# One MLP matmul or two in every open slot, gelu's ScalarE passes in halves taken from a queue, and query copies on ScalarE in mixer stage two

## The chip, the cores and the metric

The kernel runs on one core of a Trainium2 chip. The metric is device microseconds (us) of one execution. The engines are TensorE (PE, its weight loads shown as PEld), VectorE (DVE), ScalarE (ACT), GpSimd (POOL) and SyncE (SP), which only issues transfers.

## The reference

Attention of 2048 tokens over 32 heads with a given key and value cache, gated by a mixer block with an MLP; `D` is 512, `F` 1792, the inputs are bf16.

```python
xn = _layernorm(A_x)
# A: attention with cached keys and values
q = (xn @ wq) as 32 heads of 128
p = _softmax(q @ k_cache.T * 128 ** -0.5)
s = (p @ v_cache, heads side by side) @ wo
# B: mixer and MLP
h = _gelu(_layernorm(xn) @ w1)
hs = concat(four column groups of h, shifted by +1, -1, +2, -2 tokens) @ w2
x1 = xn + hs
h2 = _gelu(_layernorm(x1) @ w3) @ w4
g = _silu(x1 + h2)
return A_x + s * g
```

The gelu is the tanh approximation.

## The kernel before

Everything runs in one stream of 1024 slots, written out by the main loop (line 766). A unit is one head with 512 queries; there are 128 units (8 groups of 4 heads, 4 query tiles, 4 heads) and each has `SPU` = 8 slots. Slot `n` is slot `p = n % 8` of unit `u = n // 8`. All compute instructions are pinned to the order in which the Python code emits them, and each engine runs its own instructions in that order.

In each slot `s_slot` (line 187) emits two score matmuls, 128 keys by 512 queries each, into a PSUM tile `ps_s` of two banks, and one exponential of 1024 columns on ScalarE that turns it into half of a `pT` tile. The pool `psS` has two such tiles, so the scores of slot n+2 wait until the exponential of slot n has read its tile. `pv_slot` (line 216) emits two matmuls with the values, a lag of 5 to 10 slots behind; the lag grows by one at slots 260, 264, 268, 272 and 276, which have no value matmuls. So a slot has four matmuls of 512 columns, and some have more, here called extras:

- slots 0 and 1: two each for the queries of unit u+2 (`q_mm`, line 171; `q_copy`, line 179, brings them from the bank `xa` to SBUF in slot 2, on VectorE for nearly all units);
- slots 4 and 5: two each for the output projection (`wo_mm`, line 290), added to `s_acc` by VectorE in slot 6 (`wo_post`);
- slots 2, 3, 6 and 7, the open slots: the MLP. A window is a pair of them (2, 3 or 6, 7), numbered `w = 2u` or `2u + 1`. The MLP is a list `chunks`; each chunk has two parts, for the two slots of one window, with two matmuls each (two or three in `m4_chunk`). At the start of a window the loop compares `done` chunks with a straight line from window 10 to window 240 and takes the next chunk, or none, if the line is not passed yet.

The chunks are, in order: stage one (`m1_chunk`, h = gelu(... w1), 16 chunks), stage two (`m2_chunk`, the shifted product with w2 and the residual, 16) and, for each of four token tiles, 14 chunks of `m3_chunk` (gelu(... w3)) and 12 of `m4_chunk` (the product with w4, three chunks for each 128 tokens). All accumulate in the one bank `xm`.

`gelu_chunk` (line 502) evicts its bank on ScalarE (`pre`, line 512). After each second chunk `gelu_pair` (line 477) puts four steps on 1024 columns at fixed distances from slot n of the eviction: `square` on ScalarE one slot later, `poly` on VectorE at n+3, `tanh` on ScalarE at n+5, `last` on VectorE at n+7. `at(n, fn)` (line 134) sets a step for slot n; the loop runs a slot's steps behind its own. `soft` (line 137) moves a step to slot 3, 5 or 7 of a unit. `m4_chunk` ends with one `x2` on VectorE, a tanh on ScalarE three slots later (line 664) and `silu` on VectorE.

VectorE also sums the exponentials (lines 204 to 214), normalises the outputs (line 278 and 285), and writes the final result. POOL issues the MLP's transfers, SyncE those of attention.

Of the kernel before, what the change touches and what calls it, by code (L numbers as in the profile page):

```python
# [8 lines left out]
ACT = mybir.ActivationFunctionType  # L9
# [8 lines left out]
def kernel(  # L18
# [92 lines left out]
    o_d = {qt: dsp.tile([P, HG, 512], BF16, name=f"o_d{qt}") for qt in range(QT)}  # L111
    g_d = [dsp.tile([P, D], BF16, name=f"g_d{t}") for t in range(NT)]

    def mm(out, lhsT, rhs, start, stop):
        pin(nc.tensor.matmul(out=out, lhsT=lhsT, rhs=rhs, start=start, stop=stop))  # L115

    def rsqrt(out, var):
# [16 lines left out]
    def at(n, fn):  # L134
        todo[n].append(fn)
# [42 lines left out]

    def q_copy(u):
        qT = qtp.tile([P, 512], BF16, name="qT")  # L180
        if u > QUIET + 1:
            pin(nc.scalar.activation(out=qT[:], in_=st[u].pop("psq")[:], func=ACT.Identity))
        else:
            pin(nc.vector.tensor_copy(out=qT[:], in_=st[u].pop("psq")[:]))  # L184
        st[u]["qT"] = qT
# [287 lines left out]


    mlp = {}

    def gelu_pair(pre, dest, n):
        sq = gtp.tile([P, 2, 512], BF16, name="sq")
        f2 = "p a f -> p (a f)"

        def square():
            pin(nc.scalar.activation(  # L482
                out=sq[:], in_=pre[:], func=ACT.Square, scale=GELU_A ** 0.5))

        def poly():
            pin(nc.vector.scalar_tensor_tensor(
                out=sq[:].rearrange(f2), in0=sq[:].rearrange(f2), scalar=1.0,
                in1=pre[:].rearrange(f2), op0=ALU.add, op1=ALU.mult))

        def tanh():  # L490
            pin(nc.scalar.activation(out=sq[:], in_=sq[:], func=ACT.Tanh, scale=GELU_C))  # L491

        def last():
            pin(nc.vector.scalar_tensor_tensor(
                out=dest, in0=sq[:], scalar=1.0, in1=pre[:], op0=ALU.add, op1=ALU.mult))

        at(n + 1, square)
        at(n + 3, poly)
        at(n + 5, tanh)
        at(n + 7, last)  # L500

    def gelu_chunk(lhs, rhs, j, key, dest):
        def run(i, n):
            if i == 0:
                mlp["ps"] = psX.tile([P, 512], FP32, tag="xm", name="ps_m")
            for dc in (2 * i, 2 * i + 1):
                mm(mlp["ps"][:], lhs(dc), rhs(dc), dc == 0, dc == DC - 1)
            if i == 1:
                if j == 0:
                    mlp["pre"] = gtp.tile([P, 2, 512], BF16, name="pre")  # L510
                pre = mlp["pre"]
                pin(nc.scalar.activation(out=pre[:, j, :], in_=mlp["ps"][:], func=ACT.Identity))  # L512
                if j == 1:
                    gelu_pair(pre, dest(), n)
        return run

    ph = ExitStack()
# [32 lines left out]
    def m2_chunk(t):  # L550
        def run(i, n):
            if i == 0:
                mlp["ps"] = psX.tile([P, 512], FP32, tag="xm", name="ps_m")
                xr = mlp["xr"] = mlp.pop("xnext")
                at(n + 1 if n % SPU == 2 else n, lambda: norm1(t, xr[:], xr[:]))
                if t + 1 < NT:
                    xn_load(t + 1)
            for jc in (2 * i, 2 * i + 1):
                c0 = BASE_J[jc] + t * P - SHIFT[jc]
                mm(mlp["ps"][:], hT[:, jc, c0:c0 + P], w2_sb[:, jc, :], jc == 0, jc == DC - 1)  # L560
            if i == 1:
                ps, xr = mlp["ps"], mlp["xr"]

                def x1():
                    pin(nc.vector.scalar_tensor_tensor(
                        out=xr[:], in0=ps[:], scalar=0.5, in1=xr[:], op0=ALU.mult, op1=ALU.add))
                    nc.gpsimd.dma_start(out=x1_d[t][:], in_=xr[:])

                def stats():
                    bn = smp.tile([P, nc.vector.BN_STATS_DIM], FP32, name="bn")  # L570
                    pin(nc.vector.bn_stats(out=bn[:], in_=xr[:]))
                    pin(nc.vector.bn_aggr(out=mv2[:, t, :], in_=bn[:]))
                    rsqrt(rstd2[:, t:t + 1], mv2[:, t, 1:2])

                at(evict(n), x1)
                at(soft(n + 2), stats)
        return run

    def ph2_open():
        ph.close()  # L580
        ph2 = ph.enter_context(pool("ph2", reuse_waits="tile"))
        mlp.update(ph2=ph2, w4={}, h2={})

    def w4_load(fc):
        mlp["w4"][fc] = mlp["ph2"].tile([P, D], BF16, name=f"w4_sb{fc}")
# [25 lines left out]
    def m3_chunk(c, fc):  # L611
        def dest():
            mlp["h2"][fc // 2] = mlp["ph2"].tile([P, 2, 512], BF16, tag="h2T", bufs=FC // 2, name="h2T")
            return mlp["h2"][fc // 2][:]

        inner = gelu_chunk(
            lambda dc: mlp["w3"][:, dc, (fc % 2) * P:(fc % 2 + 1) * P],
            lambda dc: mlp["xn2T"][:, dc, :], fc % 2, None, dest)

        def run(i, n):  # L620
            if i == 0 and fc % 2 == 0:
                mlp["w3"] = mlp["w3next"].pop((c, fc))
            if i == 0 and c == 0:
                w4_load(fc)
            inner(i, n)
            if i == 1 and fc % 2 == 1:
                w3_prefetch()
        return run

    w3_order = deque((c, fc) for c in range(QT) for fc in range(0, FC, 2))  # L630
# [6 lines left out]
            pin(nc.gpsimd.dma_start(out=w[:], in_=w3_v[:, :, fc * P:(fc + 2) * P]))  # L637
            mlp["w3next"][(c, fc)] = w

    M4 = [range(0, 4), range(4, 9), range(9, 14)]  # L640

    def m4_chunk(t, part):
        fcs = list(M4[part])
        ts = t % 4

        def run(i, n):
            if part == 0 and i == 0:
                mlp["ps"] = psX.tile([P, 512], FP32, tag="xm", name="ps_m")
                mlp["xr"] = tokp.tile([P, D], BF16, tag="tb", bufs=4, name="xr")
                nc.gpsimd.dma_start(out=mlp["xr"][:], in_=x1_d[t][:])  # L650
            h = (len(fcs) + 1) // 2
            for fc in (fcs[:h], fcs[h:])[i]:
                mm(mlp["ps"][:], mlp["h2"][fc // 2][:, fc % 2, ts * P:(ts + 1) * P],
                   mlp["w4"][fc][:], fc == 0, fc == FC - 1)
            if part == 2 and i == 1:
                ps, xr = mlp["ps"], mlp["xr"]
                th = tokp.tile([P, D], BF16, tag="th", bufs=1, name="th")

                def x2():
                    pin(nc.vector.scalar_tensor_tensor(  # L660
                        out=xr[:], in0=ps[:], scalar=0.5, in1=xr[:], op0=ALU.mult, op1=ALU.add))

                def tanh():
                    pin(nc.scalar.activation(out=th[:], in_=xr[:], func=ACT.Tanh, scale=0.5))

                def silu():
                    pin(nc.vector.scalar_tensor_tensor(  # L667
                        out=xr[:], in0=th[:], scalar=1.0, in1=xr[:], op0=ALU.add, op1=ALU.mult))
                    nc.gpsimd.dma_start(out=g_d[t][:], in_=xr[:])  # L669

                at(evict(n), x2)
                at(n + 3, tanh)
                at(soft(n + 5), silu)
        return run

    chunks = deque()
# [12 lines left out]
    for c in range(QT):  # L689
        for fc in range(FC):  # L690
            chunks.append(m3_chunk(c, fc))
        if c + 1 < QT:
            hooks[len(chunks)] = lambda n, c=c: ln2(c + 1, n)
        for ts in range(4):
            for part in range(3):
                chunks.append(m4_chunk(c * 4 + ts, part))
    NCH = len(chunks)
    W0, W1 = 10, 2 * (NU - 8)
    done = 0
    window = {}  # L700


    for t, eng in enumerate([nc.sync, nc.scalar, nc.sync, nc.scalar]):
# [61 lines left out]

    for n in range(NS):
        u, p = divmod(n, SPU)
        s_slot(u, p)
        lag = next(v for lim, v in LAGS if n < lim)
        while pv_done <= n - lag:  # L770
# [14 lines left out]
        if p == 0 and u >= 1:  # L785
            add_next(u - 1, 3)
            if not turned(u - 1):
                fold(u - 1)
        if p == 2 and HG - 1 <= u < NU - 2:
            q_copy(u + 2)  # L790
        if p == 2 and u >= 1 and turned(u - 1):
            fold(u - 1)
# [31 lines left out]
            pin(nc.vector.tensor_tensor(out=a[:, 0:2, :], in0=a[:, 0:2, :], in1=a[:, 2:4, :], op=ALU.add))  # L824
        if p == 6 and u < QUIET:
            add_next(u, 2)
        if p in (2, 3, 6, 7):
            w = 2 * u + (p >= 4)
            i = p % 2
            if i == 0:  # L830
                want = -(-(w + 1 - W0) * NCH // (W1 - W0)) if w >= W0 else 0
                window.pop("run", None)
                if done < min(want, NCH):
                    if done in hooks:
                        hooks.pop(done)(n)
                    window["run"] = chunks.popleft()
                    done += 1
            if "run" in window:
                window["run"](i, n)
        for fn in todo.pop(n, ()):  # L840
            fn()
        if p == SPU - 1 and u >= 2 and turned(u - 2):
            normed(u - 2)
        if p == SPU - 1 and u == T1 + 1:
            bcast(T1)
    late = [fn for n in sorted(todo) for fn in todo[n]]
    assert min(todo) >= NS and not chunks and len(wo_todo) == 1
    U = NU - 1
# [79 lines left out]
```

## Time and profile before

| what | value |
|---|---|
| median of 3 runs | 1270.44 us (1269.98 to 1271.06) |
| span of the profiled execution | 1268.2 us |
| granted TensorE clock, mean | 0.999 |
| ACT waiting for `ps_s` scores | 122.6 us, 426 times, longest 1.1 us |
| DVE waiting for `ps_wo` (line 352) | 54.5 us, 73 times |
| DMA | 123.03 MB, mean 97 GB/s |

The profile lists, for every engine, its busy time, and for each group of instructions (line, engine, operation, output and input tiles, shape) how many there are, their busy time, the mean length of one and the idle time of the engine just before them with what ended it. `L115` is the one line that emits all matmuls, so there the tiles tell them apart. Successive instructions of an engine overlap in the records, so the time from one start to the next is shorter than the length of one. A row of the timeline has its start, its length, the engine and line, the operation and the number merged into it.

### The profile page before, as it was taken

The page shows a single profiled execution, that of the slowest core. Times are in us where ns is not written, and L with a number is a line of the kernel's source. Part 1 is how long each engine was busy: PE and PEld are TensorE (multiplying, and loading weights), DVE is VectorE, ACT ScalarE, POOL GpSimd, SP SyncE. Part 2 cuts the span into 40 slices and gives each one's busy share as a digit, 9 for nine tenths or more (in the row PEclk, how much of TensorE's full clock was granted, in tenths as well). Part 3 has the DMA queues.
Part 4 walks back from the last instruction along what each step waited for, and adds up shares of the span by engine and source line. Part 5 has one row for each costly group of instructions (what it writes and reads, how often), then busy time and mean ns, then how long its engine had stood idle before and what let it go on. Part 6 is the DMA issues. An engine that isn't in the chain of part 4 may idle for free.

```text
span 1268.2 us, 16717 instructions
## 1 busy us (share of the span) xinstructions
PE 1256.0 (99%) x5984; PEld 602.0 (47%) x5984; DVE 1091.5 (86%) x1494; ACT 1112.5 (88%) x1200; POOL 140.9 (11%) x239
## 2 busy tenths in 40 slices
PE   9999999999999999999999999999999999999998
PEld 5444444444444444444444444444444444444444
DVE  7888879898899888889898888988888899888887
ACT  7899998888999988899998889998888999988893
POOL 4420003333110010000000000000000000000111
PEclk9999999999999999999999999999999999999999
DMA  9633344355544564244554344534545344552532
GB/s 184 136 92 68 55 80 98 94 126 118 129 96 85 112 121 96 58 96 97 96 101 94 76 93 96 105 74 91 103 95 112 68 73 87 107 123 50 153 77 68
DMA packets 219876, 123.03 MB, mean 97 GB/s; under 512 B 171600, under 2 KB 196816, under 8 KB 219792
## 3 DMA queue, kind: packets, MB, share of 16 engines
q1 hardware_dynamic: 210688, 96.72, 38.9%
q0 software_dynamic: 8672, 24.91, 7.7%
q8 instruction: 46, 0.75, 0.3%
q14 instruction: 38, 0.31, 0.1%
q10 hardware_dynamic: 432, 0.33, 0.1%
HBM read 82.58 MB, written 7.60 MB: 71 GB/s over the span
## 4 chain that ended last, share of the span: by engine, by line
PE 78%; ACT 12%; DVE 7%; issue 2%; DMA 1%; POOL 0%; SPq 0%; DVEq 0%; ACTq 0%
PE ps_s L115 29%; PE ps_o L115 27%; ACT pT L198 9%; PE ps_m L115 8%; PE ps_wo L115 7%; PE ps_q L115 7%; DVE acc L209 2%; ACT pre L512 1%; ACT sq L482 1%; DMA rb<-dr 1%; ACT sq L491 1%; DVE oT L278 1%; DMA dr<-rc 1%; DVE acc L204 0%; PE ps_sum L115 0%
## 5 line engine op out<-in xcount | busy, mean ns | idle before, releaser
L198 ACT ACTIVATE pT<-ps_s 128x1024 bf16<-128x1024 f32 x1024 | 1013.0, 1033 | 132.3 <-PE ps_s L115 122.6
L115 PE MATMUL ps_s<-qT,kT 128*128 128x512 bf16 x2048 | 608.9, 379 | 2.8 <-ACT pT L198 0.9
L115 PE MATMUL ps_o<-pT,vb 128*128 128x512 bf16 x2048 | 608.2, 379 | 0.5 <-DMA vb<-in_A_v_cache_dram 0.4
L115 PEld LDWEIGHTS <-kT 128*128 128x128 bf16 x2048 | 229.8, 113 | 235.4 <-issue 23.5
L209 DVE TENSOR_TENSOR acc<-acc,pT 128x2048 bf16<-128x2048 bf16 x254 | 307.6, 1211 | 22.7 <-ACT pT L198 20.8
L115 PEld LDWEIGHTS <-vb 128*128 128x128 bf16 x2048 | 199.5, 98 | 226.2 <-DMA vb<-in_A_v_cache_dram 0.9
L204 DVE TENSOR_TENSOR acc<-pT 128x2048 bf16<-128x2048 bf16 x128 | 156.2, 1220 | 25.9 <-ACT pT L198 24.9
L115 PE MATMUL ps_q<-xnT,wq_h 128*128 128x512 bf16 (+1 forms) x524 | 152.2, 374 | 0.6 <-ACT xnT L450 0.4
L115 PE MATMUL ps_wo<-wo_h,oT 128*128 128x512 bf16 (+1 forms) x476 | 140.2, 378 | 0.0
L352 DVE TENSOR_TENSOR s_acc<-ps_wo,s_acc 128x512 f32<-128x512 f32 x100 | 68.9, 689 | 54.6 <-PE ps_wo L115 54.5
L184 DVE CAST qT<-ps_q 128x512 bf16<-128x512 f32 x122 | 83.7, 686 | 14.1 <-PE ps_q L115 14.0
L278 DVE TENSOR_TENSOR oT<-ps_o,rb 128x512 bf16<-128x512 f32 x86 | 92.2, 1073 | 1.0 <-DMA rb<-dr 1.0
L213 DVE TENSOR_TENSOR acc<-acc 128x1024 bf16<-128x1024 bf16 x127 | 87.0, 685 | 1.4
L115 PEld LDWEIGHTS <-wq_h 128*128 128x128 bf16 x524 | 50.8, 98 | 61.0 <-issue 1.2
L115 PEld LDWEIGHTS <-oT 128*128 128x128 bf16 x484 | 47.3, 98 | 56.6 <-DVE oT L285 0.5
L115 PE MATMUL ps_m<-xn2T,w_sb 128*128 128x512 bf16 x224 | 66.7, 379 | 0.0
L115 PE MATMUL ps_m<-w_sb,h2T 128*128 128x512 bf16 x224 | 64.1, 379 | 0.0
L637 POOL DMA_DIRECT2D w_sb<-in_B_w_dram x28 | 21.1, 755 | 362.0 <-PE ps_m L115 327.1
L251 DVE TENSOR_REDUCE sm<-accT 128x4 f32<-128x512 bf16 x86 | 58.6, 681 | 0.1
L214 DVE TENSOR_TENSOR acc<-acc 128x512 bf16<-128x512 bf16 x127 | 54.0, 425 | 4.4
L669 POOL DMA_DIRECT2D g_d<-xr x16 | 8.8, 547 | 319.5 <-DVE xr L667 319.5
L512 ACT ACTIVATE pre<-ps_m 128x512 bf16<-128x512 f32 x72 | 42.8, 594 | 1.3 <-PE ps_m L115 1.3
(89 smaller groups left out, 611.0 us busy)
## 6 DMA issues: line engine op xcount, KB each, us to landing
rb<-dr SPq DMA_DIRECT2D x128, 256.0 KB, 4.2
vb<-in_A_v_cache_dram SPq DMA_DIRECT2D x64, 256.0 KB, 3.9
w_sb<-in_B_w_dram POOLq DMA_DIRECT2D x28, 256.0 KB, 3.6
wo_h<-in_A_wo_dram SPq DMA_DIRECT2D x32, 128.0 KB, 3.2
wq_h<-in_A_wq_dram SPq DMA_DIRECT2D x28, 128.0 KB, 3.1
kT<-in_A_k_cache_dram SPq DMA_TRANSPOSE x128, 3.8
dr<-rc SPq DMA_DIRECT2D x128, 2.0 KB, 1.4
xr<-in_A_x_dram POOLq DMA_DIRECT2D x16, 128.0 KB, 3.7
```

The source lines that it names most:

```text
L115: pin(nc.tensor.matmul(out=out, lhsT=lhsT, rhs=rhs, start=start, stop=stop))
L184: pin(nc.vector.tensor_copy(out=qT[:], in_=st[u].pop("psq")[:]))
L198: pin(nc.scalar.activation(out=s["pT"][-1][:, jj:jj + 2, :], in_=sps[:], func=ACT.Exp, scale=SCALE))
L204: pin(nc.vector.tensor_tensor(out=s["acc"][:], in0=s["pT"][0][:], in1=s["pT"][1][:], op=ALU.add))
L209: pin(nc.vector.tensor_tensor(out=a[:], in0=a[:], in1=st[u]["pT"][i][:], op=ALU.add))
L213: pin(nc.vector.tensor_tensor(out=a[:, 0:2, :], in0=a[:, 0:2, :], in1=a[:, 2:4, :], op=ALU.add))
L214: pin(nc.vector.tensor_tensor(out=a[:, 0, :], in0=a[:, 0, :], in1=a[:, 1, :], op=ALU.add))
L251: pin(nc.vector.tensor_reduce(out=sm[:], in_=s.pop("at")[:], axis=mybir.AxisListType.X, op=ALU.add))
L278: pin(nc.vector.tensor_tensor(out=oTs[(g, qt)][:, hh, :].rearrange(f, j=4), in0=s["o"].rearrange(f, j=4), in1=s["rb"].rearrange("x (p j) - ...
L352: pin(nc.vector.tensor_tensor(out=sa, in0=ps[:], in1=sa, op=ALU.add))
L512: pin(nc.scalar.activation(out=pre[:, j, :], in_=mlp["ps"][:], func=ACT.Identity))
L637: pin(nc.gpsimd.dma_start(out=w[:], in_=w3_v[:, :, fc * P:(fc + 2) * P]))
```

## The change

It does five things.

- A chunk now counts its matmuls one by one (`run.size`: 4, or 14 for the whole of `m4_chunk`, which has no parts any more), and `run(i, n)` emits one matmul. A straight line over `NMM` = 576 matmuls tells at the start of a window how many are wanted; a window gets 2 or 4 (2 to 4 in `m4_chunk`, fewer at its end), split over its two slots.
- `square` and `tanh` of a gelu pair are emitted in two halves of 512 columns each. They go into the queue `act_late`, with the final tanh of `m4_chunk`.
- At the end of a slot at most one entry of the queue is emitted, when `debt` plus `SMALL` (2.4, in matmuls) is not over the number of extra matmuls that `ahead` names for the next two slots. `debt` rises by 2.4 with each such pass, by as much with an eviction or a query copy on ScalarE, by 0.2 with each slot (the exponential), and falls by the slot's matmuls above four.
- `poly`, `last` and `silu` follow when their inputs have been emitted, in slots 3, 5 or 7.
- While the chunks are those of stage two, `q_copy` runs on ScalarE and one slot earlier (slot 1); it does so 13 times.

```diff
     g_d = [dsp.tile([P, D], BF16, name=f"g_d{t}") for t in range(NT)]
+    mm_count = [0]
+    debt = [0.0]
+    SMALL = 2.4
+    EXP_OVER = 0.2
     def mm(out, lhsT, rhs, start, stop):
+        mm_count[0] += out.shape[-1] / 512
         pin(nc.tensor.matmul(out=out, lhsT=lhsT, rhs=rhs, start=start, stop=stop))
...
     def q_copy(u):
         qT = qtp.tile([P, 512], BF16, name="qT")
-        if u > QUIET + 1:
+        if u > QUIET + 1 or mlp.get("stage") == 2:
+            debt[0] += SMALL
             pin(nc.scalar.activation(out=qT[:], in_=st[u].pop("psq")[:], func=ACT.Identity))
...
     mlp = {}
+    act_late = deque()
...
         f2 = "p a f -> p (a f)"
-        def square():
+        def square(a):
             pin(nc.scalar.activation(
-                out=sq[:], in_=pre[:], func=ACT.Square, scale=GELU_A ** 0.5))
+                out=sq[:, a, :], in_=pre[:, a, :], func=ACT.Square, scale=GELU_A ** 0.5))
...
                 in1=pre[:].rearrange(f2), op0=ALU.add, op1=ALU.mult))
-        def tanh():
-            pin(nc.scalar.activation(out=sq[:], in_=sq[:], func=ACT.Tanh, scale=GELU_C))
+        def tanh(a):
+            pin(nc.scalar.activation(out=sq[:, a, :], in_=sq[:, a, :], func=ACT.Tanh, scale=GELU_C))
...
                 out=dest, in0=sq[:], scalar=1.0, in1=pre[:], op0=ALU.add, op1=ALU.mult))
-        at(n + 1, square)
-        at(n + 3, poly)
-        at(n + 5, tanh)
-        at(n + 7, last)
+        def squared(n):
+            square(1)
+            k = soft(n + 1)
+            at(k, poly)
+            at(k + 2, lambda: act_late.extend((lambda n: tanh(0), tanhed)))
+        def tanhed(n):
+            tanh(1)
+            at(soft(n + 2), last)
+        act_late.extend((lambda n: square(0), squared))
...
             if i == 0:
                 mlp["ps"] = psX.tile([P, 512], FP32, tag="xm", name="ps_m")
-            for dc in (2 * i, 2 * i + 1):
-                mm(mlp["ps"][:], lhs(dc), rhs(dc), dc == 0, dc == DC - 1)
-            if i == 1:
+            mm(mlp["ps"][:], lhs(i), rhs(i), i == 0, i == DC - 1)
+            if i == DC - 1:
                 if j == 0:
...
                 pre = mlp["pre"]
                 pin(nc.scalar.activation(out=pre[:, j, :], in_=mlp["ps"][:], func=ACT.Identity))
+                debt[0] += SMALL
                 if j == 1:
                     gelu_pair(pre, dest(), n)
+        run.size = DC
         return run
...
         def run(i, n):
             if i == 0:
+                mlp["stage"] = 2
                 mlp["ps"] = psX.tile([P, 512], FP32, tag="xm", name="ps_m")
...
                 if t + 1 < NT:
                     xn_load(t + 1)
-            for jc in (2 * i, 2 * i + 1):
-                c0 = BASE_J[jc] + t * P - SHIFT[jc]
-                mm(mlp["ps"][:], hT[:, jc, c0:c0 + P], w2_sb[:, jc, :], jc == 0, jc == DC - 1)
-            if i == 1:
+            c0 = BASE_J[i] + t * P - SHIFT[i]
+            mm(mlp["ps"][:], hT[:, i, c0:c0 + P], w2_sb[:, i, :], i == 0, i == DC - 1)
+            if i == DC - 1:
                 ps, xr = mlp["ps"], mlp["xr"]
...
                 at(evict(n), x1)
                 at(soft(n + 2), stats)
+        run.size = DC
         return run
...
         ph.close()
         ph2 = ph.enter_context(pool("ph2", reuse_waits="tile"))
-        mlp.update(ph2=ph2, w4={}, h2={})
+        mlp.update(stage=3, ph2=ph2, w4={}, h2={})
...
                 w4_load(fc)
             inner(i, n)
-            if i == 1 and fc % 2 == 1:
+            if i == DC - 1 and fc % 2 == 1:
                 w3_prefetch()
+        run.size = DC
         return run
...
             mlp["w3next"][(c, fc)] = w
-    M4 = [range(0, 4), range(4, 9), range(9, 14)]
-    def m4_chunk(t, part):
-        fcs = list(M4[part])
+    def m4_chunk(t):
         ts = t % 4
         def run(i, n):
-            if part == 0 and i == 0:
+            if i == 0:
                 mlp["ps"] = psX.tile([P, 512], FP32, tag="xm", name="ps_m")
                 mlp["xr"] = tokp.tile([P, D], BF16, tag="tb", bufs=4, name="xr")
                 nc.gpsimd.dma_start(out=mlp["xr"][:], in_=x1_d[t][:])
-            h = (len(fcs) + 1) // 2
-            for fc in (fcs[:h], fcs[h:])[i]:
-                mm(mlp["ps"][:], mlp["h2"][fc // 2][:, fc % 2, ts * P:(ts + 1) * P],
-                   mlp["w4"][fc][:], fc == 0, fc == FC - 1)
-            if part == 2 and i == 1:
+            mm(mlp["ps"][:], mlp["h2"][i // 2][:, i % 2, ts * P:(ts + 1) * P],
+               mlp["w4"][i][:], i == 0, i == FC - 1)
+            if i == FC - 1:
                 ps, xr = mlp["ps"], mlp["xr"]
...
                         out=xr[:], in0=ps[:], scalar=0.5, in1=xr[:], op0=ALU.mult, op1=ALU.add))
-                def tanh():
+                def tanh(n):
                     pin(nc.scalar.activation(out=th[:], in_=xr[:], func=ACT.Tanh, scale=0.5))
+                    at(soft(n + 2), silu)
...
                 at(evict(n), x2)
-                at(n + 3, tanh)
-                at(soft(n + 5), silu)
+                at(n + 3, lambda: act_late.append(tanh))
+        run.size = FC
         return run
...
             hooks[len(chunks)] = lambda n, c=c: ln2(c + 1, n)
         for ts in range(4):
-            for part in range(3):
-                chunks.append(m4_chunk(c * 4 + ts, part))
+            chunks.append(m4_chunk(c * 4 + ts))
+    NMM = sum(run.size for run in chunks)
     NCH = len(chunks)
     W0, W1 = 10, 2 * (NU - 8)
     done = 0
-    window = {}
+    mpos = 0
+    window = []
+    def ahead(n):
+        u, p = divmod(n, SPU)
+        if p in (2, 3, 6, 7):
+            return window[p % 2] if p % 2 and window else 1 if chunks and u >= W0 // 2 else 0
+        return 2
...
     for n in range(NS):
         u, p = divmod(n, SPU)
+        mm_before = mm_count[0]
         s_slot(u, p)
...
             if not turned(u - 1):
                 fold(u - 1)
-        if p == 2 and HG - 1 <= u < NU - 2:
+        if p == (1 if mlp.get("stage") == 2 else 2) and "psq" in st.get(u + 2, ()) and u >= HG - 1:
             q_copy(u + 2)
...
         if p == 6 and u < QUIET:
             add_next(u, 2)
-        if p in (2, 3, 6, 7):
+        if p in (2, 6):
             w = 2 * u + (p >= 4)
-            i = p % 2
-            if i == 0:
-                want = -(-(w + 1 - W0) * NCH // (W1 - W0)) if w >= W0 else 0
-                window.pop("run", None)
-                if done < min(want, NCH):
-                    if done in hooks:
-                        hooks.pop(done)(n)
-                    window["run"] = chunks.popleft()
-                    done += 1
-            if "run" in window:
-                window["run"](i, n)
+            want = -(-(w + 1 - W0) * NMM // (W1 - W0)) - done if w >= W0 else 0
+            window = []
+            if chunks and want > 0:
+                left = chunks[0].size - mpos
+                k = min(left, max(2, min(want, 4))) if chunks[0].size > DC else (4 if left == 4 and want >= 3 else 2)
+                window = [k - k // 2, k // 2]
+        if p in (2, 3, 6, 7) and window:
+            for _ in range(window[p % 2]):
+                if mpos == 0 and NCH - len(chunks) in hooks:
+                    hooks.pop(NCH - len(chunks))(n)
+                run = chunks[0]
+                run(mpos, n)
+                mpos += 1
+                done += 1
+                if mpos == run.size:
+                    chunks.popleft()
+                    mpos = 0
         for fn in todo.pop(n, ()):
             fn()
+        x = mm_count[0] - mm_before - 4
+        debt[0] = max(0.0, debt[0] + EXP_OVER - x)
+        if act_late and debt[0] + SMALL <= ahead(n + 1) + ahead(n + 2):
+            act_late.popleft()(n)
+            debt[0] += SMALL
         if p == SPU - 1 and u >= 2 and turned(u - 2):
...
         if p == SPU - 1 and u == T1 + 1:
             bcast(T1)
+    while act_late:
+        act_late.popleft()(NS)
     late = [fn for n in sorted(todo) for fn in todo[n]]
```

## The prediction

> **What bounds the kernel now.** I read four views in this order: the busy table, the groups by line, the waits, and the timeline of one stall.
>
> ```profile
> span 1268.2 us, 16717 instructions
> PE 1256.0 (99%) x5984; PEld 602.0 (47%) x5984; DVE 1091.5 (86%) x1494; ACT 1112.5 (88%) x1200; POOL 140.9 (11%) x239
> ...
> L198 ACT ACTIVATE pT<-ps_s 128x1024 bf16<-128x1024 f32 x1024 | 1013.0, 1033 | 132.3 <-PE ps_s L115 122.6
> L512 ACT ACTIVATE pre<-ps_m 128x512 bf16<-128x512 f32 x72 | 42.8, 594 | 1.3 <-PE ps_m L115 1.3
> L491 ACT ACTIVATE sq<-sq 128x1024 bf16<-128x1024 bf16 x36 | 39.2, 1089 | 0.0
> L482 ACT ACTIVATE sq<-pre 128x1024 bf16<-128x1024 bf16 x36 | 38.4, 1068 | 0.0
> L664 ACT ACTIVATE th<-xr 128x512 bf16<-128x512 bf16 x16 | 10.0, 623 | 0.0
> ```
>
> TensorE is busy for 99% and ScalarE still waits 122.6 us for it: on average TensorE sets the pace. Its busy share says little about what can be won, since the recorded matmuls overlap (379 ns long). So I took the starts of all 5,984 matmuls from the trace: the middle spacing is 216 ns. Priced at that pace (small ones at theirs), all delays between starts add up to 21.8 us of the span. Of these 6.6 fall in the first 40 us, which the change does not touch.
>
> I sorted the rest by what ScalarE had run between the last few exponentials. The delays whose recent ScalarE work holds a square, a gelu tanh, a final tanh or an eviction come to 10.9 us (81 delays). Delays with exponentials alone are 2.6 us, 1.3 of it between the first and last MLP matmul; row sums waiting for a VectorE copy are 2.0. One of the first kind:
>
> ```profile
> 996.69 1.07 ACT L482 ACTIVATE sq<-pre 128x1024 bf16<-128x1024 bf16 x1
> 997.64 2.96 ACT L198 ACTIVATE pT<-ps_s 128x1024 bf16<-128x1024 f32 x3
> 1000.49 0.59 ACT L512 ACTIVATE pre<-ps_m 128x512 bf16<-128x512 f32 x1
> 1000.97 1.03 ACT L198 ACTIVATE pT<-ps_s 128x1024 bf16<-128x1024 f32 x1
> 1001.87 1.07 ACT L491 ACTIVATE sq<-sq 128x1024 bf16<-128x1024 bf16 x1
> 1002.82 1.95 ACT L198 ACTIVATE pT<-ps_s 128x1024 bf16<-128x1024 f32 x2
> ```
> ```profile
> 1002.83 0.60 PE L115 MATMUL ps_s<-qT,kT 128*128 128x512 bf16 x2
> 1003.26 0.59 PE L115 MATMUL ps_o<-pT,vb 128*128 128x512 bf16 x2
> 1003.91 0.59 PE L115 MATMUL ps_s<-qT,kT 128*128 128x512 bf16 x2
> ```
>
> Two matmuls after 1003.26 the next should start at 1003.69; it starts at 1003.91, 0.05 us after the exponential of 1002.82 ends (1.03 long). The score buffer has two halves, so scores of slot n+2 wait for the exponential of slot n.
>
> **Prices, all start to start in this trace.** Matmul 0.216 us; exponential 0.903 (0.920 ahead of an eviction); eviction or query copy on ScalarE 0.476; whole square or tanh 0.946. The nearest row to a half of 512 columns is the final tanh, 0.519. First score matmul to its exponential 0.632; a single exponential takes 1.023; its end to the waiting scores 0.051. So from the scores of slot a to those of slot b+2 ScalarE needs 0.632 + 0.903 x (b-a) + inserted work + 1.023 + 0.051 when it runs without a pause.
>
> The rule tried on the old kernel: eviction after slot n, square after slot n+1, scores of n+4 (b-a = 2): 1.706 + 1.806 + 0.493 + 0.946 = 4.951 us. TensorE supplies three slots of six matmuls and, where the window behind is empty, one of four: 22 x 0.216 = 4.752. A delay of 0.20; the trace has 0.21 to 0.22 at over twenty such places.
>
> **The change, part by part.**
>
> *Dealing.* The number of matmuls is the same (the built program has as many weight loads and matmuls), so TensorE's 216 ns pace is not touched. Between slots 30 and 969 slots without any extra matmul fall from 216 to 34, counted in the two built programs. A slot of four is 0.864 us against 0.903, so back-to-back ones lose 0.039 each; I credit 1.0 of the 1.3 us (bounds 0 and 1.3).
>
> *Halves.* 72 more instructions; each pair of halves costs 2 x 0.519 - 0.946 = 0.092 us more, 72 x 0.092 = 6.6 us of ScalarE time. Hidden by the 122.6 us that ScalarE waits for scores; without that cover the 6.6 would be paid in full. What is queued behind a half is the next exponential, and behind it scores two slots on. By the rule, for the places the built program shows: eviction and half in one gap (23 times) 1.706 + 0.903 + 0.493 + 0.519 = 3.621 against slots of 5, 6, 6 = 3.672: 0.05 spare. Two tanh halves two slots apart: 3.128 against 16 matmuls, 3.456. Final tanh in a slot of six: 3.128 against 17, 3.672. Bad spots remain where slots lack their value matmuls while the lag grows (260, 264, 268, 272, 276): half after 262, eviction after 263, slot 264 of four: 1.706 + 1.806 + 0.519 + 0.493 = 4.524 for the scores of 266 against 20 matmuls, 4.320: 0.20, and the same at 274 to 278. So 0.4 us is left by the rule. The unknown is jitter at the 23 tight places and the code's assumption of two extras in slots that hold none (slots four and five of units 110 to 117). Bounds: 0.4, and half of the old 10.9, that is 5.4. I take 1.4, near the lower, since every other place has spare room.
>
> *Query copies.* 13 copies in stage two move from VectorE (13 x 0.600 off) to ScalarE: 13 x 0.476 = 6.2 us, one slot earlier. For scores of slot four after a copy at one: 1.706 + 0.903 + 0.476 + 0.017 = 3.102 against at least 16 matmuls, 3.456. Nothing on the path. It also frees the bank earlier for the row sums, whose smallest margin was 0.05 us; I credit 0 (bounds 0 and 0.5).
>
> *VectorE.* The polynomial and the last product (1.134 us each, 72 in all) move from slots two and six to three, five and seven, where they stand ahead of the eviction of the output projection (slot six) and the normalisation (end of seven). In the trace the bank is next written at least 1.48 us after that eviction, and 0.75 us after a query copy. VectorE idles some 0.13 to 0.16 us of each 1.22 us slot in the third stage; that stage gets shorter (from 14 windows of 1.69 to 22.4), which takes at most 0.01 of it. I book 0.5 us (bounds 0 and 14, below).
>
> *Queues.* Gelu results now come as late as 7 slots before their first use (12 before); 7 x 1.22 = 8.5 us covers VectorE's lag. The last gate is written one slot before SyncE loads it (two before); the next sums on that queue come four slots later. Nothing.
>
> **Sum.** 1268.2 - 10.9 - 1.0 + 1.4 + 0.5 = 1258.2 us span. The median stands 2.24 above this profile's span: 1260.4.
>
> **Rivals.** A change under 0.2% (2.5 us) I call none; the three runs before spread over 1.1.
>
> *One: stalls move, not vanish.* The halves' tight gaps (0.05 spare) fail at all 23 places and the mis-counted slots too: 5.4 us left in place of 1.4, so 1264.4. For: the margin is under the spread of an exponential (1.018 to 1.075). Against: every neighbouring gap has 0.2 or more.
>
> *Two: VectorE takes the place of ScalarE, slower.* A pass of 1.134 us ahead of the query copy eats the margin of 0.75: 0.38 us. It decides when this hits over half of 72 passes: 36 x 0.38 = 14 us, so 1274. For: VectorE at 86%, busier in stage three. Against: passes were already placed in slot six, ahead of the same normalisation.
>
> *Three: ScalarE becomes the bound.* 6.6 + 6.2 = 12.8 us more on ScalarE, all paid: 1283. Against: 122.6 us of its own waits, spread over 426 places. The page "Advanced Engine Details and Errata" of the Trainium skill (TRN2 Errata, The Read-Write Bubble) speaks for this rival: a latency stands bare between ScalarE's instructions, so it advises tiles of 512 or 1024 elements to keep the overhead small. The trace agrees that a split costs more (0.519 for a half against 0.473 for half of a whole); what the rule does not weigh is where the engine has idle time.
>
> *Four: the metering does not do what it says.* Squares stay where no slack follows: 1270. Against: the order of the built program shows halves only where the following slots hold extras, save those named.
>
> **Chances.** Forecast 0.68, one 0.14, four 0.06, two 0.09, three 0.03. Faster: forecast and one, 0.82; same 0.06; slower 0.12. The forecast's own range is 1257 to 1263. Low end of the range: all 10.9 + 1.3 and the 0.5 of the sums gained less the 0.4, 1270.44 - 12.3, with 1 us for the sums' other delays: 1257. The high end takes in rival one and a part of the same-time cases: 1268.
>
> **What would show it.** Right: delays of scores after squares fall from 10.9 to under 2 us; ScalarE's busy time up by some 15 us with its wait for scores down by about as much plus the gain; 72 squares and 72 tanh of about 0.62 us recorded each; TensorE's count unchanged at 216 ns. Wrong: delays of some 0.1 to 0.4 us behind gaps with an eviction and a half (one); TensorE waiting for VectorE's qT, s_acc or oT (two); ScalarE's wait for scores near zero (three).

## The result, and the profile after

The changed kernel takes 1258.92 us (median of 4 runs, 1258.22 to 1259.45) where the old one takes 1270.21 beside it: ratio 0.9911, 95% interval 0.9897 to 0.9925. The profiled execution spans 1257.1 us, 11.1 less than before. The forecast was a span 10.0 shorter and a median of 1260.4.

The page of the changed kernel, its span and busy table, then the chain of work that ended last, by engine, and three groups (line, engine, operation, tiles and shapes with the count | busy us, mean ns | idle before, and what ended it):

```profile
span 1257.1 us, 16639 instructions
PE 1239.8 (99%) x5866; PEld 602.4 (48%) x5984; DVE 1083.2 (86%) x1481; ACT 1130.0 (90%) x1285; POOL 145.1 (12%) x239
...
PE 94%; DVE 2%; DMA 2%; issue 1%; ACT 1%; SPq 0%; POOL 0%; DVEq 0%; POOLq 0%
```
```profile
L207 ACT ACTIVATE pT<-ps_s 128x1024 bf16<-128x1024 f32 x1024 | 1024.0, 1028 | 104.1 <-PE ps_s L123 89.1 <-PE ps_q L123 2.2 <-PE ps_wo L123 1.9
L492 ACT ACTIVATE sq<-pre 128x512 bf16<-128x512 bf16 x72 | 45.7, 635 | 0.0
L501 ACT ACTIVATE sq<-sq 128x512 bf16<-128x512 bf16 x72 | 45.1, 626 | 0.0
```

ScalarE works 17.5 us more (1130.0 against 1112.5) and the kernel is faster. The chain runs through ScalarE for 1% now. Before, it was 12%:

```profile
PE 78%; ACT 12%; DVE 7%; issue 2%; DMA 1%; POOL 0%; SPq 0%; DVEq 0%; ACTq 0%
```

ScalarE's idle time before its exponentials was 132.3 us and is 104.1. The 28.2 us less are about the extra work and the time that the kernel no longer takes, 17.5 + 11.1. The part of it put down to scores, in us, times and longest:

```profile
ACT pT L207 <- PE ps_s L123: 89.1, 321, 1.1
```

It was 122.6 and fell by 33.5, more than the 28.2, because 4.1 us now stand under `ps_q` and `ps_wo`. In this profile 118 records of matmuls are missing (5,866; the 5,984 weight loads are all there), which look like delays of exactly one matmul. So I read delays between matmul starts from a second profile of the same kernel (`e10_changed_again`, span 1256.6), which has them all:

| delays between matmul starts, us (their number) | before | changed |
|---|---|---|
| all | 21.8 | 9.8 |
| scores behind squares, tanh, evictions | 10.85 (81) | 0.85 (6) |
| scores, exponentials alone, slots 42 to 969 | 1.6 | 0.1 |
| row sums waiting for VectorE's query copy | 2.0 | 1.6 |

A gelu pair in that second profile, from ScalarE's timeline:

```profile
981.87 0.60 ACT L528 ACTIVATE pre<-ps_m 128x512 bf16<-128x512 f32 x1
982.35 2.09 ACT L207 ACTIVATE pT<-ps_s 128x1024 bf16<-128x1024 f32 x2
984.33 0.62 ACT L492 ACTIVATE sq<-pre 128x512 bf16<-128x512 bf16 x1
984.85 1.96 ACT L207 ACTIVATE pT<-ps_s 128x1024 bf16<-128x1024 f32 x2
986.71 0.62 ACT L492 ACTIVATE sq<-pre 128x512 bf16<-128x512 bf16 x1
987.23 1.96 ACT L207 ACTIVATE pT<-ps_s 128x1024 bf16<-128x1024 f32 x2
989.46 2.10 ACT L207 ACTIVATE pT<-ps_s 128x1024 bf16<-128x1024 f32 x2 [0.27 <-PE ps_s L123]
```

Each half stands between exponentials and takes 0.52 us from start to start (984.33 to 984.85); two exponentials separate them. At 989.46 ScalarE waits for scores again: the backlog is gone. In the old timeline a whole square, the next eviction and a whole tanh stood within 5.2 us (996.69 to 1001.87) and TensorE ended up waiting.

### The profile page after: what moved, and what is told of

It reads as the page before. It is cut to its first block, busy times and chain, and to the rows that moved or that the text cites. A ratio compares the mean times of both kernels' runs of the same rounds, so it can differ in the third digit from the quotient of the medians.

```text
span 1257.1 us, 16639 instructions
## 1 busy us (share of the span) xinstructions
PE 1239.8 (99%) x5866; PEld 602.4 (48%) x5984; DVE 1083.2 (86%) x1481; ACT 1130.0 (90%) x1285; POOL 145.1 (12%) x239
## 4 chain that ended last, share of the span: by engine, by line
PE 94%; DVE 2%; DMA 2%; issue 1%; ACT 1%; SPq 0%; POOL 0%; DVEq 0%; POOLq 0%
PE ps_o L123 34%; PE ps_s L123 33%; PE ps_m L123 10%; PE ps_wo L123 8%; PE ps_q L123 8%; DMA xin<-in_A_x_dram 1%; PE ps_sum L123 0%; DVE acc L218 0%; ACT pT L207 0%; DMA dr<-rc 0%; DMA vb<-in_A_v_cache_dram 0%; SPq L158 0%; DMA rb<-dr 0%; DVE bn L384 0%; DVE gf L338 0%
## 5 line engine op out<-in xcount | busy, mean ns | idle before, releaser
L207 ACT ACTIVATE pT<-ps_s 128x1024 bf16<-128x1024 f32 x1024 | 1024.0, 1028 | 104.1 <-PE ps_s L123 89.1
L123 PE MATMUL ps_o<-pT,vb 128*128 128x512 bf16 x2012 | 600.1, 379 | 4.7 <-DMA vb<-in_A_v_cache_dram 0.7
L123 PE MATMUL ps_s<-qT,kT 128*128 128x512 bf16 x1992 | 596.9, 379 | 2.2 <-ACT qT L481 0.4
L193 DVE CAST qT<-ps_q 128x512 bf16<-128x512 f32 x109 | 74.9, 687 | 7.3 <-PE ps_q L123 6.4
L123 PE MATMUL ps_m<-w_sb,h2T 128*128 128x512 bf16 x221 | 76.1, 379 | 0.1
L123 PE MATMUL ps_m<-xn2T,w_sb 128*128 128x512 bf16 x218 | 75.3, 379 | 0.3
L496 DVE SCALAR_TENSOR_TENSOR sq<-sq,pre 128x1024 bf16<-128x1024 bf16 x36 | 43.8, 1217 | 3.4 <-ACT sq L492 3.4
```

The costliest lines, as they stand in the source:

```text
L207: pin(nc.scalar.activation(out=s["pT"][-1][:, jj:jj + 2, :], in_=sps[:], func=ACT.Exp, scale=SCALE))
L496: pin(nc.vector.scalar_tensor_tensor(out=sq[:].rearrange(f2), in0=sq[:].rearrange(f2), scalar=1.0, in1=pre[:].rearrange(f2), op0=ALU.add, ...
```

## The experiments

Times are medians; every one has runs of the old kernel beside it (1269.3 to 1269.5). My theory: the place and length of a ScalarE pass against the matmuls behind it decide.

**Dealing alone** (`e1_deal_only`).

```diff
-        if u > QUIET + 1 or mlp.get("stage") == 2:
+        if u > QUIET + 1:
...
-        act_late.extend((lambda n: square(0), squared))
+        at(n + 1, square)
+        at(n + 3, poly)
+        at(n + 5, tanh)
+        at(n + 7, last)
...
```

> The dealing of matmuls alone: whole squares and tanh at their old fixed slots, query copies on VectorE. Theory (the length and place of a ScalarE pass against the matmuls behind it decide): a square one slot after an eviction needs 4.95 us to the scores of n+4; slots of 5, 6, 6, 5 matmuls supply 4.75, so the 0.2 us delay stays at most of the 36 pairs (some 7 us); only the delays of back-to-back slots without extras go. About 1266 us, ratio to before 0.996 to 0.999. Rival (empty open slots were the cause, dealing does it all): 1259 to 1260 us, ratio 0.991.

1264.98 us, ratio 0.9966 (0.9953 to 0.9978), within the expected ratio. The plain delays fall to 0.1 us; 5.7 of the 10.85 us behind gelu passes stay, 23 delays instead of 81. One of these, 0.97 us at 667.19, is a wait for a load of keys (`kT`) and no gelu's. So dealing alone is worth some 4 us (4.3), and about half of the gelu delays go with it. The expectation had 0.2 us at most of the 36 squares, pricing all of them by four slots with 22 matmuls. In this build 7 squares have 22, one has 21 and 28 have 23 (4.97 us, against the 4.95 needed). The trace has 0.22 us at those 7, 0.44 at the one and no delay at the 28: the rule holds to 0.02 us, the count was wrong.

**Halves, queue and metering alone** (`e2_halves_only`). The old kernel with the new `gelu_pair`, `debt` and queue, and an `ahead` for its windows:

```diff
...
+        if p in (2, 3, 6, 7):
+            if n == now[0] + 1 and p % 2:
+                return 2 if "run" in window else 0
+            return 2 if done < wanted(2 * u + (p >= 4)) else 0
+        return 2
...
```

> Halves, queue and metering alone: chunks keep their two parts and windows, so 216 open slots stay without extras; query copies on VectorE. Theory: halves are put only where the next two slots hold extras (eviction and half need 3.62 us against 18 matmuls, 3.89), so most of the 10.9 us goes, and only the 2.6 us of delays among plain exponentials stay: 1260 to 1262 us, ratio 0.992 to 0.994. Rival (without the dealing there is no room for the halves): they pile up at the full windows and 1265 us or more is measured, ratio over 0.996.

1261.33 us, 0.9935 (0.9921 to 0.995). Delays behind gelu passes are 1.4 us and the plain ones stay at 1.6. The larger part of the gain, some 8 us, needs no dealing.

**Whole passes in the queue's first places** (`e3_whole_queued`).

```diff
+            debt[0] += WHOLE - SMALL
...
-        act_late.extend((lambda n: square(0), squared))
+        act_late.append(square)
```

> The changed kernel with whole squares and tanh, put where the queue would put the first half and booked at 4.4 matmuls. Theory: an eviction and a whole square in one gap need 4.05 us against 5, 6, 6 matmuls (3.67): 0.38 us at some 23 places, and 0.1 at others, 8 to 10 us in all: about 1267 us, ratio 0.996 to 0.999. Rival (the metering is what counts, halving is not needed): 1259 to 1260 us, ratio 0.991.

1276.64 us, 1.0059 (1.0044 to 1.0074): slower than the old kernel, and more than I expected. ScalarE's and TensorE's timelines at one place:

```profile
400.13 0.59 ACT L525 ACTIVATE pre<-ps_m 128x512 bf16<-128x512 f32 x1
400.75 1.06 ACT L493 ACTIVATE sq<-pre 128x1024 bf16<-128x1024 bf16 x1
401.71 3.79 ACT L208 ACTIVATE pT<-ps_s 128x1024 bf16<-128x1024 f32 x4
```
```profile
401.81 0.59 PE L124 MATMUL ps_q<-xnT,wq_h 128*128 128x512 bf16 x2
402.77 0.59 PE L124 MATMUL ps_s<-qT,kT 128*128 128x512 bf16 x2 [0.36 <-ACT pT L208]
```

The scores should start at 402.24 (two matmuls behind 401.81) and start at 402.77, 0.53 late. The square starts 0.62 us after the eviction, not 0.476, as at all 34 places of this build where a square stands directly behind an eviction. A whole tanh there, as long as the square but of another pair, starts 0.48 after it (7 times):

```profile
547.38 0.59 ACT L525 ACTIVATE pre<-ps_m 128x512 bf16<-128x512 f32 x1
547.86 1.06 ACT L506 ACTIVATE sq<-sq 128x1024 bf16<-128x1024 bf16 x1
```

So it isn't the length: the square reads what this eviction writes, and starts about when the eviction (0.59 long) ends. With 0.623 for 0.476 the sum is 4.19 us. This build has 34 such gaps, 21 with 17 matmuls behind (3.672) and 13 with 18 (3.888): 21 x 0.52 + 13 x 0.31 = 15.0 us. The trace has 14.7 in 34 delays three slots behind. The sum I had made took 23 gaps and no wait. All delays behind gelu passes come to 19.8 us. The run shows that whole passes in these places cost time. It doesn't show that halving is needed: whole passes metered at their own size and kept away from their eviction were not run, and in `e1_deal_only` whole squares one slot behind the eviction are late at only 8 of 36 places.

**Copies of stage two on VectorE** (`e4_copy_dve`).

```diff
-        if u > QUIET + 1 or mlp.get("stage") == 2:
+        if u > QUIET + 1:
...
-        if p == (1 if mlp.get("stage") == 2 else 2) and "psq" in st.get(u + 2, ()) and u >= HG - 1:
+        if p == 2 and "psq" in st.get(u + 2, ()) and u >= HG - 1:
```

> The changed kernel with the 13 query copies of stage two back on VectorE in slot two. Theory (the copies are worth nothing by themselves): within 1 us of the changed kernel, ratio 0.991 to 0.992; at most 0.1 us each where the row sums wait for the copy. Rival (the copies carry a part of the gain): 1261 us or more.

1258.14 us, 0.991 (0.9895 to 0.9925). The copies are worth nothing that can be told: one row sum comes 0.29 us late in stage two (262.29), directly after VectorE's copy of the queries.

**No metering** (`e5_no_meter`).

```diff
-        if act_late and debt[0] + SMALL <= ahead(n + 1) + ahead(n + 2):
+        if act_late:
```

> The changed kernel with the queue unmetered: one entry at the end of each slot, whatever follows. Theory: every first half of a square stands in the gap of its eviction (36 places, 21 before) and the second one slot later; to the scores four slots on ScalarE then needs 1.706 + 1.806 + 0.493 + 1.038 = 5.04 us against 5, 6, 6, 5 matmuls (4.75): 0.29 us at most of 36 places, 7 to 10 us: 1266 to 1268 us. Rival (short passes are enough, the metering adds nothing): 1258 to 1260 us.

1264.6 us, 0.9962 (0.9947 to 0.9977): 5.7 us slower than the changed kernel's first median and 6.3 than its second (below), half of its gain lost, less than the 7 to 10 expected. The built order explains the squares: of the 36 places only 8 have 22 matmuls or fewer in the four slots, 28 have 23 (4.97 us), so the same rule gives 28 x 0.075 + 7 x 0.29 + 0.51 = 4.6 us. The trace has 4.9 there, in 34 delays. I had priced all places by the poorest supply. I had also left out the tanh: the delays behind gelu passes come to about 8 us in all, 3 of them behind tanh.

**Quarters** (`e6_quarters`), 144 more instructions.

```diff
+            for b in (slice(0, 256), slice(256, 512)):
+                pin(nc.scalar.activation(
+                    out=sq[:, a, b], in_=pre[:, a, b], func=ACT.Square, scale=GELU_A ** 0.5))
...
```

> The changed kernel with every half in two quarters, emitted back to back: 144 more ScalarE instructions, by the price of a split (0.092 us) 13 us more ScalarE time in the same places. Theory (ScalarE time is hidden where slack follows, paid where it does not): half plus 0.09 at the 23 tight places (0.05 spare) gives 0.04 us each, 1 us, and up to 1 more: 1259 to 1261 us. Rival (ScalarE sets the pace, each added instruction is paid): 1272 us.

1260.08 us, 0.9927 (0.991 to 0.9943). A quarter takes 0.306 us from start to start, so each split costs 0.092 once more, 13.2 us in all, of which 1.2 to 1.8 (from the changed kernel's medians 1258.92 and 1258.32 to 1260.08) are paid. The intervals overlap, but the trace shows where: behind 19 gaps with an eviction and a half the scores now come 0.05 us late, and there is no such delay in the changed kernel. The rule left 0.05 to spare there, and 0.09 was added. ScalarE is not the bound; its wait for scores shrinks instead:

```profile
ACT pT L207 <- PE ps_s L123: 81.2, 290, 1.1
```

**Lag grown in stage two** (`e7_turn_stage2`, on top of `e4_copy_dve`).

```diff
-    T0, T1 = 8 * HG, NU - 10
+    T0, T1 = 7 * HG, NU - 10
```

> Query copies on VectorE as in e4_copy_dve, and the growth of the lag (slots without value matmuls) four units earlier, where the MLP is still in stage two and no gelu runs. Theory: the delays left between 320 and 345 us, 0.5 us in e4_copy_dve, go; four units sum their rows by transposing instead of by small matmuls, 0.13 us each: 1 us less than e4_copy_dve. Rival (those delays come with the growing lag itself, wherever it stands): no difference.

1256.75 us, 0.9899 (0.9885 to 0.9914). The delays in the slots where the lag grows are gone (five in `e4_copy_dve`, 0.55 us). So is the one of 0.30 at slot 302; one of 0.22 stands at slot 270 instead, in TensorE's timeline:

```profile
331.55 0.59 PE L123 MATMUL ps_o<-pT,vb 128*128 128x512 bf16 x2
332.20 0.59 PE L123 MATMUL ps_s<-qT,kT 128*128 128x512 bf16 x2
```

It is the delay of slot 302, moved with the growth of the lag (the slots are explained below, under the rule). This is the fastest kernel run, though its interval overlaps those of the changed kernel (0.991, 0.9895 to 0.9924 in its second run), so the time alone does not show it to be faster than that.

**The same near the start of stage two** (`e8_turn_early`, `T0 = 5 * HG`).

> As e7_turn_stage2, but the growth twelve units earlier than in the changed kernel, near the start of stage two. Theory: the same 0.5 us, and twelve units without the small matmuls, 12 x 0.13 = 1.5 us: 2 us less than e4_copy_dve, about 1256. Rival (VectorE, which takes 0.68 us more in each of these units, becomes late in stage two): new waits for VectorE's row sums or queries, 1258 us or more.

1257.78 us, 0.9911 (0.9896 to 0.9926). No gain over `e7_turn_stage2`. The time is just under the rival's 1258 us, but its mechanism is there, if not in the instruction that it named: TensorE's next MLP chunk waits for VectorE's residual `xr` (us, times, longest).

```profile
PE ps_m L123 <- DVE xr L583: 1.4, 2, 0.8
```

**Early copies on ScalarE** (`e9_early_copy`, on top of `e7_turn_stage2`). The edit also takes the copies of the first units, before unit 3.

```diff
-        if u > QUIET + 1:
+        if u > QUIET + 1 or u <= HG + 5:
...
-        if p == 2 and "psq" in st.get(u + 2, ()) and u >= HG - 1:
+        if p == (1 if u <= HG + 3 else 2) and "psq" in st.get(u + 2, ()) and u >= HG - 1:
```

> As e7_turn_stage2, with the query copies of units 3 to 7 (ahead of most MLP work) on ScalarE and one slot earlier. Theory: the row sums at about 37 and 54 us, which wait 0.3 and 0.8 to 1.3 us for VectorE's query copy, start at once: 1 to 1.6 us less than e7_turn_stage2, about 1255.5. Rival (the VectorE work behind the copy is late in any case, or the exponentials, which run back to back there, pay 0.476 us for each copy): no gain, or up to 2 us more.

1257.84 us, 0.9905 (0.9889 to 0.9922). The wait of the row sums at 38 us is gone and that at 57 us is 0.7 instead of 1.3, now for VectorE's `acc`. But a new delay of 0.5 us appears at 21 us, and queries wait for ScalarE's copy 1.6 us in all. No gain.

**The changed kernel again** (`e10_changed_again`).

> The changed kernel once more, beside e9_early_copy on the same chip: 1258 to 1260 us. Theory: its delays after gelu passes stay under 1.2 us in a second profile, most of them between 320 and 345 us, and the single wait of VectorE for the broadcast rb at 444 us (3.0 us long) does not come back, being a transfer's. Rival: that wait belongs to the changed order and is there again.

1258.32 us, 0.991 (0.9895 to 0.9924). The rival holds for the wait at 444 us: in VectorE's timeline it is there again.

```profile
444.02 1.07 DVE L287 TENSOR_TENSOR oT<-ps_o,rb 128x512 bf16<-128x512 f32 x1 [2.61 <-DMA rb<-dr]
```

It costs TensorE 0.37 us here, 0.55 in the first profile (0.77 less a missing record). The other traces have it too wherever the matmuls are dealt, `e1_deal_only` included, and neither the old kernel nor `e2_halves_only` has it there: it comes with the dealing. The first profile's chain shows the small store `dr` taking 3.02 us (its median to landing is 1.4), and the broadcast `rb` issued behind it 3.92 (median 4.2). SyncE issues that store 0.64 us after a weight load (437.24 to 437.88), in the old kernel 2.92 after it (434.60 to 437.52). Whether that makes the store slow was not tried.

## Why the prediction was right

*What bounded the kernel.* Right. Of the 12.0 us of delays that are gone, 10.0 were behind gelu passes, and undoing either main part brings a share back (`e1_deal_only` 4.7 us of them, without the wait for keys; `e2_halves_only` 1.4 of gelu and 1.6 of plain delays).

*The rule for ScalarE against the matmuls behind.* Right to 0.02 us in `e1_deal_only`, and to 0.02 to 0.05 at the two bad spots named for the growing lag, which were given 0.20 each. The first (half after 262, eviction after 263) in TensorE's timeline of the second profile:

```profile
326.82 0.59 PE L123 MATMUL ps_s<-qT,kT 128*128 128x512 bf16 x2
327.25 0.59 PE L123 MATMUL ps_q<-xnT,wq_h 128*128 128x512 bf16 x2
327.80 0.59 PE L123 MATMUL ps_s<-qT,kT 128*128 128x512 bf16 x2
328.23 0.59 PE L123 MATMUL ps_o<-pT,vb 128*128 128x512 bf16 x2
328.66 0.59 PE L123 MATMUL ps_q<-xnT,wq_h 128*128 128x512 bf16 x2
329.20 0.59 PE L123 MATMUL ps_s<-qT,kT 128*128 128x512 bf16 x2
```

Scores at 327.80 instead of 327.68 and at 329.20 instead of 329.09: 0.12 and 0.11, 0.22 in sum, the scores of slots 265 and 266. The second spot has 0.14 and 0.11; a delay of 0.07 at slot 261 was not foreseen. The tight gaps with 0.05 to spare, for which the forecast kept a part of another 1.0 us, gave way nowhere, and `e6_quarters` shows that the spare was no larger. The other part of that 1.0 was for slots whose extras `ahead` counts though they aren't there. Outside the growing lag one delay is left, 0.30 us at slot 302, and it is of this kind:

```profile
369.58 0.59 PE L123 MATMUL ps_s<-qT,kT 128*128 128x512 bf16 x2
370.02 0.59 PE L123 MATMUL ps_o<-pT,vb 128*128 128x512 bf16 x2
370.45 0.59 PE L123 MATMUL ps_s<-qT,kT 128*128 128x512 bf16 x2
370.88 0.59 PE L123 MATMUL ps_o<-pT,vb 128*128 128x512 bf16 x2
371.61 0.59 PE L123 MATMUL ps_s<-qT,kT 128*128 128x512 bf16 x2
```

Slots 300 and 301, slots four and five of unit 37, hold no output projection, so they have four matmuls each where `ahead` counts two extras. A half square (368.59) and an eviction (370.01) were put ahead of them. By the rule that is 4.524 against 20 matmuls, 4.320: 0.20. The prediction named units 110 to 117 for this and missed unit 37. With the lag grown four units earlier the two slots are 268 and 269, and the delay stands at 270 (`e7_turn_stage2`). So rival one fell, and the term "left over" was 0.85 instead of 1.4: 0.55 in the growing lag and 0.30 here.

*Dealing.* Credited 1.0, measured 1.5. The size was off: delays among plain exponentials between slots 42 and 969 are 1.6 us, not the 1.3 stated, and nearly all of them went. The account was also too simple: the prediction gave the gelu delays to the halves alone, while dealing by itself removes about half of them. `e1_deal_only` (4.3 us) and `e2_halves_only` (8.0) together make more than the 11.3 of both in one.

*Halves cost nothing.* A half takes 0.52 us from start to start, as the final tanh that priced it. 0.092 us per split make 6.6 us, hidden by ScalarE's own waits. `e6_quarters` shows it, since twice as much again costs 1.2 to 1.8 us. That disposes of rival three. The Trainium skill ("Advanced Engine Details and Errata", The Read-Write Bubble) advises tiles of 512 or 1024 elements to keep the overhead small; the halves, of 512, still keep to that, and only the quarters fall below. The traces agree that a split costs, 0.092 us each, which the kernel pays mostly in time that ScalarE would have waited.

*Query copies.* Booked 0, `e4_copy_dve` shows 0.

*VectorE.* Booked 0.5 us, and none of it was needed. In the second profile no wait of TensorE for a query copy or the output projection appears after slot 48 apart from 0.1 us or less, at slot 968; rival two fell for this change, though `e8_turn_early` shows that VectorE has little room in stage two.

*Queues.* "Nothing" was wrong by 0.4 to 0.55 us: the broadcast at 444 us, on a path that the prediction did not look at.

*The sum.* The span of the second profile is 1256.6 us, 1.6 under the 1258.2 forecast. That is 0.55 in the halves, 0.5 in the dealing, 0.5 for VectorE and 0.4 in the row sums, which no term had, less the 0.4 of the broadcast. Nearly all errors point one way, so the hit owes little to errors that cancel.

*Metering.* Rival four fell: the delays behind gelu passes are 0.85 us, though in unit 37 the metering does count what isn't there. Without it some 6 us are lost (`e5_no_meter`).

## What to carry to other kernels

When one engine is busy 99% and another feeds it through a buffer of two, look at the starts, not at busy time, and compare for each inserted pass what the feeder needs up to the second next buffer with what the other engine has to do until then. Cutting a pass in two costs the fixed part once more, and is paid back where each part fits in the slack that follows. Count the places in the built order before multiplying: the sums that missed here (for `e1_deal_only`, `e3_whole_queued` and `e5_no_meter`) went wrong in the count or the supply; in `e3_whole_queued` a price was wrong too, in `e5_no_meter` the tanh were left out.

## What the runs showed that I had not expected

Halving has a second effect. A half that reads only the first eviction starts 0.477 us after the start of the second one (21 times in the second profile); the whole square reads both and starts 0.623 after it (34 times in `e3_whole_queued`). Queued directly behind the eviction, whole passes therefore cost 0.15 us more each than their length tells.
